# A tile of its own for the ring's last slot, and a new order for every engine, in a fused attention and MLP kernel

## The chip, the cores and the metric

The kernel runs on one core of a Trainium2 chip. The metric is device time in microseconds (us): the median of three runs was 1024.15 us (1023.66 to 1025.81).

Five engines work side by side, each through its own queue in order: TensorE (PE, with PEld for its weight loads), VectorE (DVE), ScalarE (ACT), GpSimd (POOL) and SyncE (SP), which here only issues transfers (DMA). An instruction that waits holds up all that stands behind it on its engine.

## The reference

Eight batches of eight heads go through a linear attention with exponential features; its output, as 4608 tokens of 512 numbers, goes through two dense layers with a squared ReLU between them.

```python
def phi(x):                                   # x: (8, 8, 576, 64), w_phi: (64, 128)
    proj = np.einsum('bhsd,df->bhsf', x, w_phi)
    proj = proj - np.max(np.abs(proj), axis=-1, keepdims=True)
    return np.concatenate([np.exp(proj), np.exp(-proj)], axis=-1)
q_p, k_p = (phi(q), phi(k))
kv = np.einsum('bhsf,bhsd->bhfd', k_p, v)
z = np.sum(k_p, axis=2)
num = np.einsum('bhsf,bhfd->bhsd', q_p, kv)
den = np.einsum('bhsf,bhf->bhs', q_p, z)[..., None] + 1e-06
x = (num / den).transpose(0, 2, 1, 3).reshape(4608, 512)
h = x @ w_in                                  # w_in: (512, 2048)
r = np.maximum(h, 0.0)
return (r * r) @ w_out                        # w_out: (2048, 512)
```

## The kernel before

**Attention.** The 64 heads go in 32 pairs p. Loads of k, q and v (L524, L525, L487) are issued by SP. The first six pairs (`early`) do it all on PE, DVE and ACT: products for keys and queries (L532, L538, L655, L661), the largest absolute value and its subtraction on DVE (L548 to L562, L666, L668), exponentials on ACT (L554, L556), key by value (L594, L599, L627), turns (L639, L689), numerators (L708) and denominators (L725). The other 26 pairs (`visit`, `late`) take other routes: L809, L818, L830 on PE, and POOL for the largest value (L906) and the denominators' sum (L927). For each batch the scale needs the largest of v: ACT L493, DVE L498, then PE L341 (`power`).

**Weights.** The 16 pieces of w_in and w_out (`raw0i` to `raw7o`, L383) come in during the first 110 us. ACT, POOL (L402) and DVE (L406) turn each into two or three parts of lower precision.

**Token ring.** The attention's output is split into a high and a low f16 part (L783, L786) and lies in a ring of eight slots of 256 tokens each, T = 256. In the code, `ring[0]` holds slots 0 to 2 and `ring[1]` slots 3 to 7, one tile of shape [128, 2, 4, 1280]:

```python
def place(slot, t=0):
    half = slot * T >= HR
    return int(half), slot * T + t - HR * half
```

**Dense layers.** The tokens go in 18 chunks of 256. Chunks 0 to 3 (`moe`) take the first product straight (L956, 24 matmuls for each of eight pieces f, reading the ring), and `ph` through the ReLU (ACT L965 or DVE L967) to squares `gh`, `gl` (L973, L975, L249), then the second product (L993, 12 matmuls into `po`). From chunk 4 on they go in pairs of chunks with seven products in place of eight (`step`, L1161, 42 matmuls each; sums on DVE L1167 and L1119). That needs block sums of w_in: `ahead` makes them for all eight f while chunks 0 to 3 are computed, with slot 7 of the ring as its workspace (DVE L1075, L1060, L249; ACT L1079 or DVE L1080; store L1082). They are loaded back by `weights` (L1091, L1093) for each step. Finished `po` banks are scaled into `o` by ACT (L1016) or DVE (L1014) and stored.

**Order.** All work is added to a plan as items, each with an engine, a length, and for a transfer two numbers (`xfer`, `land`). Two strings of digits, ORDER and WAYS, were found by annealing against that plan. ORDER gives the order in which all items are issued, WAYS the engine of each item that may run on several. The kernel doesn't reorder anything at run time. Where the plan shows PE idle, a few matmuls on zeros (`zeros`, L1332) are put in.

Of the kernel before, what the change touches and what calls it, by code (L numbers as in the profile page):

```python
# [26 lines left out]
F = 128  # L27
# [153 lines left out]
def place(slot, t=0):  # L181
    half = slot * T >= HR
    return int(half), slot * T + t - HR * half
# [52 lines left out]
def tile_kernel(ctx, tc, qp, kp, vp, w_phi, w_in, w_out, out):  # L236
# [30 lines left out]
    ring = [[cp.tile([128, KT, HR], F16, name=f"ring0_{i}") for i in range(2)], None]  # L267
# [57 lines left out]
    ld_w = P.add("SP", 0.45, lambda: SP.dma_start(wraw, w_phi), [], [], -100.0, land=2.2, xfer=0.5)  # L325
# [160 lines left out]
    def load_v(p, rank):  # L486
        v_load[p] = P.add("SP", 0.47, lambda: SP.dma_start(v_at(p), vp[p]), [], [v_key(p)], rank, land=2.4, xfer=1.0 if p < 2 else 0.8)  # L487
# [35 lines left out]
    def loads(p, rank):  # L523
        k_load[p] = P.add("SP", 0.47, lambda: SP.dma_start(k_[p], kp[p]), [], [("k", p)], rank, land=2.4, xfer=1.0 if p < 2 else 0.72)  # L524
        q_load[p] = P.add("SP", 0.47, lambda: SP.dma_start(q_[p], qp[p]), [], [("q", p)], rank + 0.5, land=2.4, xfer=0.9 if p < 1 else 0.72)  # L525
# [79 lines left out]
    def early(p):  # L605
# [113 lines left out]
        def dens():  # L719
# [16 lines left out]
            R(5.7), land=2.1, xfer=0.1)  # L736
# [4 lines left out]
    def denominators(p, dens, rows, rank):  # L741
# [5 lines left out]
        o = P.add("SP", 0.4, lambda: SP.dma_start(rd_[p], rc_[p]), [o], [("rc", p), ("rd", p)], rank, land=2.4, xfer=0.1)  # L747
# [3 lines left out]
    def spread(p, o, rows, rank):  # L751
# [4 lines left out]
        dens_of[p] = P.add("SP", 1.3, work, [o], [("rd", p), ("rb", p)], rank, land=2.1, xfer=0.8)  # L756
# [118 lines left out]
    def turn(p, v, key, src, rank):  # L875
# [3 lines left out]
            td_[p].rearrange("s p x -> p s x"), kvs_[p][:, 0:256].rearrange("p (s x) -> p s x", s=2)), [o], [("kvs", p), ("td", p)], rank, land=1.9, xfer=0.1)  # L879
# [3 lines left out]
            [o], [("td", p), ("kz", p)], rank, land=2.2, xfer=0.5)  # L883

    def late(p):
# [4 lines left out]
        w = P.add("SP", 0.4, lambda: SP.dma_start(zd_[p], z4_[p]), sums[p], [("z4", p), ("zd", p)], R(RZ), land=1.9, xfer=0.1)  # L890
# [12 lines left out]
        for h in range(2):  # L903
# [27 lines left out]
                [home, ("den", p)], R(RQ + 1.0), land=2.4, xfer=0.1))  # L931
# [73 lines left out]
    def store(c, v, i, use, bank, g2, Q):  # L1005
# [14 lines left out]
        for k, x in enumerate([slice(0, DM)]):  # L1020
# [6 lines left out]
                  land=1.8, xfer=0.7)  # L1027
# [37 lines left out]
    def ahead(f, rank):  # L1065
# [4 lines left out]
        for k in range(2):  # L1070
            of = lambda x, h, k=k: w_[f][0][:, x, 2 * h + k, :].rearrange("p (j c) -> p j c", j=2)

            def fill(of=of):
                for h in range(2):
# [8 lines left out]
                      [o], [], rank, land=2.0, xfer=0.8)  # L1083
# [5 lines left out]
    def weights(f, rank):  # L1089
        b = in_pair["step"] = in_pair.get("step", 1) ^ 1  # L1090
        o = P.add("SP", 0.45, lambda: SP.dma_start(wo_at(b), wd_[f][0]), [w_stored[f]] + read_o[b], [WO[b]], rank, land=2.4, xfer=1.8)  # L1091
        if f in s_stored:
            s = P.add("SP", 0.45, lambda: SP.dma_start(ws_at(b).rearrange("p k n x c -> p k (n x c)"), wd_[f][1]), s_stored[f] + read_s[b], [WS[b]], rank, land=2.4, xfer=1.8)  # L1093
# [16 lines left out]
        s_stored[f] = [P.add("SP", 0.45, lambda: SP.dma_start(wd_[f][1], ws_at(b).rearrange("p k n x c -> p k (n x c)")), [s], [WS[b]], rank, land=2.0, xfer=1.4)]  # L1110
# [110 lines left out]
    def put_away(n, k, f, g, rank):  # L1221
# [4 lines left out]
        gone[k, f] = P.add("SP", 0.9, work, [g] + read_back.get((k - 2, f), []), [("gh", n), ("gl", n)], rank, land=2.2, xfer=1.9)  # L1226

    def take_back(n, k, f, rank):
# [4 lines left out]
        o = P.add("SP", 0.9, work, [gone[k, f]], [("gh", n), ("gl", n)], rank, land=2.4, xfer=1.6)  # L1233
# [64 lines left out]
    for k, cs in enumerate(PAIRS):  # L1298
# [3 lines left out]
        for i in range(2):  # L1302
            add_x(cs, i, used, m - 6.0 + 0.5 * i, None if k else RT[0])
# [61 lines left out]
    "#m#s$+$/$3#B#R#z#X#|$:$M$O$%$;$?$d$s$v%,%1%0%:%;%A%F%Y%[%n%}&&&+![#[#6#d#A#E$$$1#H#L#p$-#u#w$)$I$<$K"
    "$V$h$m$4$b$k$o$r$y%#%&%+%-%/%6%@%C%^&%%t&*%O%U%X%g%k%y&.&4&8!d!^#;$D#F#Q$!$Z&f(%(+(b)A#U$=#h$2$#$.$N"
    "$W$&$9$B$F$7$8$J$L$q$z%(%?%L%%%2%=%7%>%E%J%K%d%i%o%q%z&!&6&;&D&`&(&-&1&=&@&S&q)%))(n).#n${$E$a$P$Y$j"
    "%5$S$^$e$p$f$i$u%e%T%h%p&,&<&2&?&M&I&P&C&_&a&T&[&^&c&h&k(1(5(I(P(D(N(Q(e(h)*)>)S)q)V)s$@%_%H%B%Q%R%`"
    "%x%V%Z%f%l%N%c%]%v%|&#&)%I&v(8&o%{(>(@(F&p&y(^&u&}(((0(&(2(6(G&5(,($(J(B(K(c&Z(o(t)<(s({)!)&)?)C)F)Y"
# [107 lines left out]
```

## Time and profile before

| | |
|---|---|
| median of three runs | 1024.15 us |
| the profiled execution | 1026.95 us |
| its span, first to last instruction | 1025.1 us |
| PE busy | 999.6 us, 98% |
| DVE / ACT / POOL busy | 799.8 / 604.3 / 357.1 us |
| mean granted PE clock | 0.991 of full speed |

The profiled execution is 2.8 us above the median; 1.85 us of it lie around the span. Idle time in a row below is what an engine waited before an instruction, with what ended the wait behind the arrow. A busy PE is modelled from the ends of pipelined matmuls.

### The profile page before, as it was taken

What the parts mean: (1) busy time and instruction counts of PE and PEld (TensorE: products, weight loads), DVE (VectorE), ACT (ScalarE), POOL (GpSimd) and SP (SyncE); (2) the same over time, 40 slices, a digit from 0 to 9 for tenths busy, and PEclk for the clock granted to TensorE, in tenths of its full rate; (3) what the DMA queues carried; (4) which work ended last, traced back from release to release, by engine and by line L of the source; (5) the groups of instructions that cost most, each with busy time, mean ns of one, the idle gap of its engine ahead of it and who ended that gap; (6) DMA issues with size and microseconds to landing.
All of it is one profiled execution on the core that took longest, in us unless ns stands there. A gap on an engine that the chain in (4) does not pass through costs nothing.

```text
span 1025.1 us, 19857 instructions
## 1 busy us (share of the span) xinstructions
PE 999.6 (98%) x7548; PEld 679.8 (66%) x7548; DVE 799.8 (78%) x1407; ACT 604.3 (59%) x1131; POOL 357.1 (35%) x144
## 2 busy tenths in 40 slices
PE   7999999999999999999999999999999999999998
PEld 4656666666667776677657776677667757767674
DVE  5898789899798788988789888777897776672443
ACT  5888766677554478377764876456735642440423
POOL 1562355565420064444274444431543420000000
PEclk9899999999999999999999999999999999999999
DMA  8863433564225576679476776757656765674321
GB/s 314 289 208 126 148 81 108 146 172 134 46 67 169 192 231 165 215 215 266 155 207 184 213 236 179 226 165 239 166 148 197 218 187 197 194 255 143 110 93 42
DMA packets 155687, 180.60 MB, mean 176 GB/s; under 512 B 76872, under 2 KB 105544, under 8 KB 153544
## 3 DMA queue, kind: packets, MB, share of 16 engines
q1 hardware_dynamic: 155304, 178.81, 57.2%
q8 instruction: 59, 0.97, 0.4%
q10 hardware_dynamic: 288, 0.52, 0.1%
q14 instruction: 36, 0.29, 0.1%
HBM read 137.93 MB, written 41.21 MB: 175 GB/s over the span
## 4 chain that ended last, share of the span: by engine, by line
PE 80%; DVE 7%; DMA 5%; issue 3%; ACT 2%; POOL 2%; SPq 1%; POOLq 0%; DVEq 0%; ACTq 0%
PE po L993 30%; PE ph L1161 10%; PE pn L1161 6%; PE pv L1161 6%; PE ph L956 6%; PE pz L594 4%; PE pn L830 3%; PE pp L1161 2%; PE pn L809 2%; PE pp L532 2%; PE pv L830 2%; DMA q<-in_qp_dram 1%; DMA rb<-rd 1%; PE pz L599 1%; PE pv L993 1%
## 5 line engine op out<-in xcount | busy, mean ns | idle before, releaser
L1161 PEld LDWEIGHTS <-w 128*128 128x128 f16 x2352 | 224.3, 98 | 48.4 <-issue 20.7
L906 POOL PARTITION_ALL_REDUCE mx<-pt x52 | 116.1, 2233 | 204.9 <-ACT pt L253 119.0
L993 PE MATMUL po<-wh,gh 128*128 128x512 f32 x544 | 175.2, 443 | 0.0
L927 POOL PARTITION_ALL_REDUCE rb<-rb x26 | 97.2, 3740 | 161.9 <-DVE rb L924 154.4
L993 PE MATMUL po<-wl,gh 128*128 128x512 bf16 x544 | 141.0, 381 | 1.8 <-DVE o L1014 1.5
L1212 ACT ACTIVATE w<-w,cw 128x512 f32<-128x512 f32 x112 | 78.6, 714 | 107.7 <-DVE w L1167 107.7
L993 PE MATMUL po<-wl,gl 128*128 128x512 bf16 x544 | 140.4, 380 | 0.6 <-DVE gl L249 0.4
L993 PEld LDWEIGHTS po<-wh,gh 128*128 128x128 f32 x544 | 103.3, 190 | 31.8 <-issue 0.3
L927 POOL PARTITION_ALL_REDUCE ds<-ds x26 | 96.1, 3698 | 39.1 <-DVE ds L924 20.8
L973 ACT ACTIVATE gh<-w 128x512 fp32r<-128x512 f32 x112 | 69.9, 625 | 62.4 <-PE po L993 30.0
L993 PEld LDWEIGHTS <-gl 128*128 128x128 bf16 x576 | 56.3, 98 | 69.2 <-DVE gl L249 1.6
L249 DVE TENSOR_TENSOR gl<-w,gh 128x512 bf16<-128x512 f32 x112 | 80.6, 727 | 23.9 <-ACT w L975 23.1
L956 PE MATMUL ph<-ring,w 128*128 128x256 f16 x768 | 91.1, 276 | 2.8 <-DVE r L967 2.3
L993 PEld LDWEIGHTS <-gh 128*128 128x128 bf16 x576 | 51.2, 98 | 59.4 <-issue 21.5
L956 PEld LDWEIGHTS <-w 128*128 128x128 f16 x768 | 73.5, 99 | 22.9 <-issue 12.1
L1161 PE MATMUL ph<-ring,w 128*128 128x256 f16 x624 | 85.6, 273 | 0.0
L1161 PE MATMUL pv<-w,w 128*128 128x256 f16 x576 | 70.7, 273 | 0.3 <-ACT pt L253 0.3
L580 DVE TRANSPOSE_TENSOR_REDUCE z<-e 128x32 f32<-128x1024 f32 x52 | 64.0, 1233 | 3.8 <-ACT e L556 3.2
L1167 DVE TENSOR_TENSOR w<-pv,w 128x512 f32<-128x512 f32 x96 | 53.1, 553 | 10.2 <-PE pv L1161 8.1
L554 ACT ACTIVATE e<-e 128x512 f32<-128x512 f32 x64 | 39.5, 622 | 29.3 <-DVE e L551 29.2
L249 DVE TENSOR_TENSOR qe<-pt,mx 128x576 f32<-128x576 f32 x52 | 45.6, 878 | 10.1 <-POOL mx L906 5.5
L1167 DVE TENSOR_TENSOR w<-pn,w 128x512 f32<-128x512 f32 x48 | 32.9, 686 | 23.3 <-PE pn L1161 14.1
(256 smaller groups left out, 1835.3 us busy)
## 6 DMA issues: line engine op xcount, KB each, us to landing
w<-wd SPq DMA_DIRECT2D x112, 512.0 KB, 4.4
gd<-gh SPq DMA_DIRECT2D x48, 256.0 KB, 4.2
gh<-gd SPq DMA_DIRECT2D x48, 256.0 KB, 3.2
v<-in_vp_dram SPq DMA_DIRECT2D x32, 320.0 KB, 3.9
q<-in_qp_dram SPq DMA_DIRECT2D x32, 288.0 KB, 4.0
k<-in_kp_dram SPq DMA_DIRECT2D x32, 288.0 KB, 3.7
rb<-rd SPq DMA_DIRECT2D x64, 144.0 KB, 3.6
out_dram<-o SPq DMA_DIRECT2D x34, 256.0 KB, 4.1
```

The source lines that it names most:

```text
L249: eng.tensor_tensor(out=out_, in0=a, in1=b_, op=ALU.subtract)
L580: sums[p].append(P.add("DVE", dve_us(256 * k), lambda: V.tensor_reduce(out=col(), in_=src().rearrange("p k (b x) -> p k b x", x=32), op=AL ...
L594: PE.matmul(out=to[64 * h:64 * h + 64, 0:256], lhsT=v_at(p)[:, t, h, :], rhs=e_[2 * p + h][:, t].rearrange("p s f -> p (s f)"), start=t == ...
L830: PE.matmul(out=to[64 * h:64 * h + 64, :], lhsT=kz_[n][:, 128 * s_ + 64 * h:128 * s_ + 64 * h + 64], rhs=qe_[2 * n + h].rearrange("p (s x) ...
L906: o = P.add("POOL", par_us(S), lambda n=n, h=h: G.partition_all_reduce(mx_[n - EARLY], pt_[p][:, h, :], channels=128, reduce_op=bass_isa.R ...
L927: o = P.add("POOL", 3.6, lambda y=y: G.partition_all_reduce(y(), y(), channels=128, reduce_op=bass_isa.ReduceOp.add), [o], [home], R(RQ + ...
L956: PE.matmul(out=ph[:, j, :], lhsT=w_[f][0][:, w, t, 128 * j:128 * j + 128], rhs=at_ring(c, x, t), start=k == 0, stop=k == 3 * KT - 1)
L973: sq = P.add("ACT", act_us(512), lambda: A.activation(out=gh_[n], in_=r(), func=AF.Square), after, use + [("gh", n)], Q)
L993: PE.matmul(out=bank(i), lhsT=x[:, j, 128 * i:128 * i + 128], rhs=w[:, j, :], start=turn + j + s == 0, stop=(turn, j, s) == (NFP - 1, 1, 2))
L1161: PE.matmul(out=to, lhsT=fl(x, *al)(k), rhs=fr(y, *ar)(k), start=n == 0, stop=n == 5)
L1167: V.tensor_tensor(out=to, in0=a, in1=b, op=ALU.add)
L1212: x = P.add("ACT", act_us(512, 1), lambda i=i: A.activation(out=r()[:, 2 * i:2 * i + 2, :], in_=r()[:, 2 * i:2 * i + 2, :], func=AF.Relu, ...
```

## The change

It has five parts.

1. Slot 7 of the ring becomes a tile of its own (`ring[2]`, shape [128, 2, 4, 256]); `ring[1]` keeps slots 3 to 6. A pair's output that crosses from slot 6 to slot 7 is now cut in two there, which is the case for batches 3 and 6: eight more high and eight more low pieces.
2. The lengths that the plan gives to transfers (`xfer`, `land`) are new numbers. They change no instruction by themselves.
3. In `add_x` of the first pair of chunks the second half waits for the first.
4. ORDER and WAYS are new throughout.
5. WAYS moves some items: `wh` casts (L442) from POOL 7 to 4 and on DVE 1 to 3, `wl` casts (L460) on POOL 2 to 4, scaling of `po` on ACT (L1016) 20 to 24 and on DVE (L1014) 14 to 10. Zero matmuls (L1332) go from 10 to 14, and four of them now stand right behind PE's first eight (L359).

```diff
 def place(slot, t=0):
-    half = slot * T >= HR
-    return int(half), slot * T + t - HR * half
+    half = (slot * T >= HR) + (slot == RING // T - 1)
+    return half, slot * T + t - (0, HR, RING - T)[half]
...
-        whole = late_pool.tile(
-            [128, 2, KT, RING - HR], F16, name="ring1")
-        ring[1] = [whole[:, i] for i in range(2)]
+        for x, size in ((1, RING - HR - T), (2, T)):
+            whole = late_pool.tile([128, 2, KT, size], F16, name=f"ring{x}")
+            ring[x] = [whole[:, i] for i in range(2)]
...
-        k_load[p] = P.add("SP", 0.47, lambda: SP.dma_start(k_[p], kp[p]), [], [("k", p)], rank, land=2.4, xfer=1.0 if p < 2 else 0.72)
+        k_load[p] = P.add("SP", 0.47, lambda: SP.dma_start(k_[p], kp[p]), [], [("k", p)], rank, land=1.85, xfer=1.02)
...
-        o = P.add("SP", 0.45, lambda: SP.dma_start(wo_at(b), wd_[f][0]), [w_stored[f]] + read_o[b], [WO[b]], rank, land=2.4, xfer=1.8)
+        o = P.add("SP", 0.45, lambda: SP.dma_start(wo_at(b), wd_[f][0]), [w_stored[f]] + read_o[b], [WO[b]], rank, land=1.9, xfer=1.76)
...
-            add_x(cs, i, used, m - 6.0 + 0.5 * i, None if k else RT[0])
+            add_x(cs, i, used + ([] if k or not i else [parts_x[cs, 0]]), m - 6.0 + 0.5 * i, None if k else RT[0])
...
-    "!&!#!!!(!)!4!:!1!6!O!_!j!m!p!s)x!+!J!I!P!S!7!X!W!a!v#K#N#T#c#g#k!Y#!!{#(#-#5#J!>#&!i#+#1###j#P#q#v#{"
+    "!$!#!!!(!)!+!9!4!=!M!`!e!g!j$7&q!,!P!N!V![!-!X!W!^!w#>#B#]#d#I#p!a#!###)#-#4#M!?#&!p#,#1!{#o#S#u#y$!"
```

**Place 1: SP's first transfers.** Before, SP's queue begins like this (`raw0i`, `raw1i`, `raw2i` are pieces of w_in):

```order
L525 DMA q_167<-in_qp_dram 128x576
L524 DMA k_169<-in_kp_dram 128x576
L325 DMA wraw<-in_w_phi_dram 128x768
L487 DMA v_172<-in_vp_dram 128x640
L487 DMA v_174<-in_vp_dram 128x640
L524 DMA k_176<-in_kp_dram 128x576
L383 DMA raw0i<-in_w_in_dram 128x2048
L524 DMA k_218<-in_kp_dram 128x576
L487 DMA v_220<-in_vp_dram 128x640
L383 DMA raw1i<-in_w_in_dram 128x2048
L487 DMA v_231<-in_vp_dram 128x640
L383 DMA raw2i<-in_w_in_dram 128x2048
```

The next row is the load of the second pair's q. Of the change:

```order
L325 DMA wraw<-in_w_phi_dram 128x768
L525 DMA q_168<-in_qp_dram 128x576
L524 DMA k_170<-in_kp_dram 128x576
L487 DMA v_172<-in_vp_dram 128x640
L487 DMA v_174<-in_vp_dram 128x640
L524 DMA k_176<-in_kp_dram 128x576
L487 DMA v_178<-in_vp_dram 128x640
L383 DMA raw0i<-in_w_in_dram 128x2048
L383 DMA raw1i<-in_w_in_dram 128x2048
L524 DMA k_225<-in_kp_dram 128x576
L487 DMA v_232<-in_vp_dram 128x640
L525 DMA q_235<-in_qp_dram 128x576
```

`wraw` now goes first, `raw1i` stands ahead of the third k (whose buffer must first be read by PE), and the second q stands ahead of `raw2i`.

**Place 2: DVE in `ahead`, while PE computes chunk 3 from slot 3.** Before, with the semaphores that each instruction waits for in brackets (`w_0_1242` is a piece of w_in, `ring_1719` the tile of slots 3 to 7):

```order
L551 TENSOR_TENSOR e_3458<-pp_3424,km_3456 128x4x128 [waits DVE_49]
L1075 TENSOR_TENSOR ring_1719<-w_0_1242 128x2x128 [waits PE_49] x2
L761 TENSOR_TENSOR rb_3033<-n_3234,rb_3033 128x576 [waits DMAHW1_49,DMAHW0_49]
L1060 TENSOR_TENSOR ring_1719<-ring_1719 128x128 [waits DVE_49]
L249 TENSOR_TENSOR ring_1719<-ring_1719 128x128 [waits DVE_49] x3
L786 SCALAR_TENSOR_TENSOR ring_1719<-rb_3033,cb,ring_1719 128x576 [waits Activation_49]
```

Of the change, at the same step (`ring_1682` is slot 7's own tile, `ring_1681` holds slots 3 to 6):

```order
L249 TENSOR_TENSOR qe_3476<-pt_3310,mx_3403 128x576 [waits Pool_49]
L1075 TENSOR_TENSOR ring_1682<-w_0_1248 128x256 x2
L1060 TENSOR_TENSOR ring_1682<-ring_1682 128x128 [waits DVE_49]
L249 TENSOR_TENSOR ring_1682<-ring_1682 128x128 [waits DVE_49] x3
L898 TENSOR_REDUCE zc_3504<-kz_3405 128x4 [waits DMAHW5_49,DMAHW0_49]
L551 TENSOR_TENSOR e_3506<-pp_3412,km_3443 128x4x128
L786 SCALAR_TENSOR_TENSOR ring_1681<-rb_2959,cb,ring_1681 128x576 [waits Activation_49]
```

Of the 32 instructions of L1075, 13 waited for PE before, and none does now. In the other direction, 14 matmuls that read slots 3 to 6 waited for one of L1075 before, and none does now.

**Place 3: DVE and ACT where the last pair with put-away squares ends (about 911 to 919 us).** Before, DVE:

```order
L976 TENSOR_TENSOR w_1_4086<-w_1_4086 128x512
L249 TENSOR_TENSOR gl_10855<-w_1_4086,gh_10849 128x512
L249 TENSOR_TENSOR gl_10870<-w_1_4086,gh_10853 128x512
L249 TENSOR_TENSOR r<-r 128x256 x4
L1053 CAST w_1_3656<-r 128x1024
L1014 TENSOR_SCALAR o_10887<-po_10348,cc 128x512
```

DVE of the change, and behind it ACT of the change:

```order
L249 TENSOR_TENSOR gl_10875<-w_1_4083,gh_10869 128x512
L249 TENSOR_TENSOR gl_10890<-w_1_4083,gh_10873 128x512
L249 TENSOR_TENSOR r<-r 128x256 x4
L1053 CAST w_1_3742<-r 128x1024
L249 TENSOR_TENSOR w_1_3742<-r,w_1_3742 128x1024
```

```order
L973 ACTIVATE gh_10873<-w_1_4083 128x512
L975 ACTIVATE w_1_4083<-w_1_4083 128x512
L1016 ACTIVATE o_10902<-po_10367,cc_79 128x512
L1016 ACTIVATE o_10909<-po_10370,cc_79 128x512
L1052 ACTIVATE w_1_3882<-r 128x1024
```

Before, ACT scaled the first of these two `po` banks and DVE the second, behind the sums for the next pair; now ACT scales both, one after the other.

Two more moves on PE: around 20 us the second pair's eight L655 now stand ahead of L639 and L341, which before came first, and around 39 us four numerator matmuls (L708) now stand between L538 and L661, which before followed each other directly.

## Rows read from the trace of the kernel before

**Rows 1.** The page's first part: busy us, share of span, instructions, per engine.

```profile
PE 999.6 (98%) x7548; PEld 679.8 (66%) x7548; DVE 799.8 (78%) x1407; ACT 604.3 (59%) x1131; POOL 357.1 (35%) x144
```

**Rows 2.** Windows: stretch, its us, busy us per engine, clock, DMA share, GB/s.

```profile
150.00:200.00 50.00, 48.68 (x378) 33.46 (x377) 46.31 (x83) 32.61 (x67) 27.33 (x10) 1.00 0.43 120
400.00:500.00 100.00, 99.96 (x738) 67.53 (x735) 88.03 (x151) 66.27 (x131) 44.96 (x15) 1.00 0.71 214
```

**Rows 3.** Windows of PE alone: stretch, its us, PE busy, clock, DMA, GB/s.

```profile
7.00:14.00 7.00, 6.83 (x58) 0.76 0.79 296
24.00:29.00 5.00, 5.00 (x39) 0.66 1.03 419
41.00:47.00 6.00, 5.94 (x46) 0.72 0.50 107
86.00:90.00 4.00, 2.36 (x28) 1.00 0.24 74
287.00:291.00 4.00, 4.00 (x22) 0.57 0.01 4
918.50:923.00 4.50, 4.50 (x15) 0.62 0.80 273
```

**Rows 4.** Waits of PE, whole span: us in total, times, longest.

```profile
PE pn L341 <- DVE m L498: 2.8, 2, 1.6
PE ph L655 <- DMA wraw<-in_w_phi_dram: 2.4, 1, 2.4
PE ph L956 <- DVE r L967: 2.3, 3, 1.6
PE pn L725 <- ACT n L253: 1.6, 1, 1.6
PE po L993 <- DVE o L1014: 1.5, 1, 1.5
...
PE pn L538 <- DVE pt L668: 1.0, 1, 1.0
PE pn L661 <- DVE et L562: 1.0, 1, 1.0
...
PE ph L655 <- DMA q<-in_qp_dram: 0.5, 1, 0.5
```

**Rows 5.** The chain that ended last, 0 to 30 us: start, us, what.

```profile
1.64 5.09 DMA wraw<-in_w_phi_dram
...
13.09 10.78 DMA q<-in_qp_dram
```

**Rows 6.** Timeline of DVE around 21 us.

```profile
21.11 1.23 DVE L406 SCALAR_TENSOR_TENSOR u<-u,raw1i 128x1024 int32<-128x1024 int32 x1 [1.53 <-POOL raw1i L402]
...
22.72 0.15 DVE L498 TENSOR_REDUCE m<-vm 128x1 f32<-128x4 f32 x1
```

**Rows 7.** Timeline of DVE, 278 to 288 us.

```profile
278.21 0.42 DVE L1075 TENSOR_TENSOR ring<-w 128x256 f32<-128x256 f16 x1 [1.99 <-PE ph L956]
...
284.90 0.75 DVE L967 TENSOR_SCALAR r<-ph,cw 128x512 f32<-128x512 f32 x1
285.57 1.01 DVE L1075 TENSOR_TENSOR ring<-w 128x256 f32<-128x256 f16 x1
```

**Rows 8.** Timelines of PE and POOL there.

```profile
286.63 0.60 PE L956 MATMUL ph<-ring,w 128*128 128x256 f16 x4 [0.42 <-DVE ring L1075]
...
283.46 3.90 POOL L927 PARTITION_ALL_REDUCE rb<-rb  x1 [7.61 <-DVE rb L924]
```

**Rows 9.** Timelines of ACT, DVE and PE, 915 to 919 us.

```profile
915.29 0.69 ACT L1016 ACTIVATE o<-po,cc 128x512 f32<-128x512 f32 x1 [1.11 <-PE po L993]
...
917.27 0.81 DVE L1014 TENSOR_SCALAR o<-po,cc 128x512 f32<-128x512 f32 x1
...
918.12 0.38 PE L993 MATMUL po<-wl,gh 128*128 128x512 bf16 x1 [1.50 <-DVE o L1014]
```

**Rows 10.** Transfers: times issued, KB each, median us from issue to landing.

```profile
w<-wd SPq DMA_DIRECT2D x112, 512.0 KB, 4.4
```

More of the change, by code (lines that the diff above doesn't have):

```diff
@@ L266, in tile_kernel @@
     wout = [[None] * 3 for _ in range(NFP)]
-    ring = [[cp.tile([128, KT, HR], F16, name=f"ring0_{i}") for i in range(2)], None]
+    ring = [[cp.tile([128, KT, HR], F16, name=f"ring0_{i}") for i in range(2)], None, None]
     cc = cp.tile([128, NT // 128], F32, name="cc")
@@ L323, in tile_kernel @@
         V.memset(mask[64 * h:64 * h + 64, h, :], 1.0)
-    ld_w = P.add("SP", 0.45, lambda: SP.dma_start(wraw, w_phi), [], [], -100.0, land=2.2, xfer=0.5)
+    ld_w = P.add("SP", 0.45, lambda: SP.dma_start(wraw, w_phi), [], [], -100.0, land=1.7, xfer=1.36)
     pool_start = P.add("POOL", 10.8, lambda: None, [], [], -100.0)
@@ L735, in early @@
             den_[p], dn()[0:128:32, :].rearrange("j (r x) -> j r x", x=9)), [o], use + [("den", p)],
-            R(5.7), land=2.1, xfer=0.1)
+            R(5.7), land=1.5, xfer=0.1)
         rows = lambda h: rd_[p].rearrange("(c h r) x -> h c (r x)", c=2, h=2)[h].unsqueeze(0).to_broadcast([64, 2, SH])
@@ L754, in work @@
                 SP.dma_start(rb_[p][64 * h:64 * h + 64, :].rearrange("p (c x) -> p c x", c=2), rows(h))
-        dens_of[p] = P.add("SP", 1.3, work, [o], [("rd", p), ("rb", p)], rank, land=2.1, xfer=0.8)
+        dens_of[p] = P.add("SP", 1.3, work, [o], [("rd", p), ("rb", p)], rank, land=1.85, xfer=1.7)
     def tokens(p, nums, rank):
@@ L888, in late @@
         R = lambda x: rank + x
-        w = P.add("SP", 0.4, lambda: SP.dma_start(zd_[p], z4_[p]), sums[p], [("z4", p), ("zd", p)], R(RZ), land=1.9, xfer=0.1)
+        w = P.add("SP", 0.4, lambda: SP.dma_start(zd_[p], z4_[p]), sums[p], [("z4", p), ("zd", p)], R(RZ), land=1.25, xfer=0.36)
         back = []
@@ L1026, in store @@
             P.add("SP", 0.38, lambda x=x: (SP if whole else A).dma_start(out[128 * tt:128 * tt + 128, x], home(x.start)), [o], [mine], Q,
-                  land=1.8, xfer=0.7)
+                  land=1.35, xfer=0.6)
     parts_x, in_pair = {}, {}
@@ L1082, in ahead @@
             o = P.add("SP", 0.45, lambda k=k: SP.dma_start(wd_[f][1].rearrange("p x (n c) -> p x n c", n=4)[:, k], ring[spot][1][:, :, c0:c0 + T]),
-                      [o], [], rank, land=2.0, xfer=0.8)
+                      [o], [], rank, land=1.35, xfer=0.8)
             in_pair["ahead"] = [o]
@@ L1224, in work @@
             SP.dma_start(gd_[k % 2][f][1], gl_[n])
-        gone[k, f] = P.add("SP", 0.9, work, [g] + read_back.get((k - 2, f), []), [("gh", n), ("gl", n)], rank, land=2.2, xfer=1.9)
+        gone[k, f] = P.add("SP", 0.9, work, [g] + read_back.get((k - 2, f), []), [("gh", n), ("gl", n)], rank, land=1.5, xfer=1.2)
     def take_back(n, k, f, rank):
@@ L1231, in work @@
             SP.dma_start(gl_[n], gd_[k % 2][f][1])
-        o = P.add("SP", 0.9, work, [gone[k, f]], [("gh", n), ("gl", n)], rank, land=2.4, xfer=1.6)
+        o = P.add("SP", 0.9, work, [gone[k, f]], [("gh", n), ("gl", n)], rank, land=1.5, xfer=1.42)
         read_back[k, f] = [o]
@@ L1365 @@
[L1365 to L1369, printed above, removed]
```

177 lines of the change are left out of this document (91 added, 86 removed).

## The prediction

> **What bounds the kernel now.** I read the engines' totals first: PE is busy for 999.6 of 1025.1 us, and the next engine, DVE, for 78% [rows 1]. The windows say that this is no average over unlike stages: between 400 and 500 us PE is idle for 0.04 us, and even at 150 to 200 us, while weights and attention are still being prepared, for 1.3 us [rows 2]. So nearly every part of the program is bound by PE's own stream of matmuls, which the change doesn't shorten. What it can move is the 25.5 us in which PE stands idle, and what they bring with them.
>
> What they bring is seen in windows over PE alone [rows 3]. In five stretches the granted clock is below full speed; 7 to 14 us ran at 0.76, which loses 0.24 x 7.0 = 1.7 us, and the other four lose 0.34 x 5 = 1.7, 0.28 x 6 = 1.7, 0.43 x 4 = 1.7 and 0.38 x 4.5 = 1.7 us. Of TensorE's two levels, 2.4 and 1.2 GHz, the chip granted the lower one for a part of each, and the sum is 8.5 us. What PE did before each is in its waits [rows 4]: 2.4 us for `wraw`; 1.6 us at L341, with the second q after it; 1.0 and 1.0 us at L661 and L538; 1.6 us behind L967 with 0.42 us more [rows 8]; 1.5 us at L993. The single wait of 1.6 us at L725 was followed by full clock (86 to 90 us) [rows 3, 4]. So a wait that is near another, or longer than this one, costs about 1.7 us beside itself, and one of up to 1.6 us that stands alone does not.
>
> **The change part by part.**
>
> *Start.* `wraw` was issued at 1.64 us and landed 5.09 us later [rows 5]; PE waited 2.4 us for it [rows 4]. It now goes first in SP's queue, two issues earlier. A transfer's place decides what shares the way with it: only `wraw` and q must land before PE's L655, k no longer. The gain is between 0 (all three land together as before) and 1.6 us (`wraw` leaves at the span's start); I take 0.7, which is k's part of the three (576 of 1920 words a partition) of the 2.4 us. Four zero matmuls stand in the wait that is left; at the 0.38 us of a 128x512 matmul [rows 9] they last 1.5 us, so the wait covers them, and if it shrank to nothing they would cost that. With PE occupied for most of it I expect the low clock at 7 to 14 us to be shorter: 0 to 1.7, taken as 1.2. Sum 1.9.
>
> *Around 21 us.* PE waited 1.6 us at L341 for DVE's L498, which ended at 22.87 us; DVE stood before it in L406 until the part of `raw1i` was there (1.53 us idle, then 1.23 us of work) [rows 4, 6]. `raw1i` now passes one k and one v in SP's queue. The k waits for a buffer that PE reads, so this is more than two issues; how far ahead it comes is bounded by the transfers on the way. The second q landed 10.78 us after its issue [rows 5], behind `raw1i` and `raw2i`, of which one is now behind it and the other well ahead; and L655 covers the rest of PE's wait. The wait of 1.6 and the 0.5 for q [rows 4] can go, and 1.7 of low clock with them: 0 to 3.8, taken as 3.0, because L341 still comes after a join of `raw1i` on DVE.
>
> *Around 39 us.* Two waits of 1.0 us, at L661 and L538 [rows 4]. Four L708 now stand in the first; the second has nothing new in front of it. If a single one is left, the low clock of 41 to 47 us should go too, by what L725 showed. 0 to 2.7, taken as 1.7.
>
> *The ring's last slot.* PE waited 1.6 us for L967 on DVE, and 0.42 us more for an L1075 of `ahead` [rows 4, 8]. L967 started at 284.90, in line behind items that had slid back when DVE stood idle for 1.99 us at 278.21, waiting for PE's L956 [rows 7]. L956 reads slot 3 and L1075 writes slot 7; they share nothing but the tile. The two engines thus waited for each other in turn, and with a tile apart neither does. Had DVE not lost those 1.99 us, L967 would have started about 2 us earlier, more than PE's 1.6. It could gain the 0.42 alone, or 1.6 + 0.4 + 1.7 of clock = 3.7; I take 2.7, since DVE's line there is a new one.
>
> *End of the last put-away pair.* PE waited 1.5 us for a `po` bank that DVE scaled at 917.27, while ACT had scaled the other from 915.29 to 915.98 [rows 9]. Both are now ACT's, one behind the other: the second would end at about 915.98 + 0.69 + a hop, some 916.7 in place of 918.08, so 1.3 of the 1.5 go, and 1.7 of low clock [rows 3]. 0 to 3.2, taken as 2.8.
>
> *What costs nothing.* Eight more cuts of the ring make eight more DVE and ACT pieces, each shorter than L967's 0.75 us [rows 7], and three or four weight items move from POOL to DVE, of 1.2 us or less as L406 [rows 6]. Their cover is DVE's spare time, 12 us in 100 at 400 us, 3.7 in 50 at 150 us [rows 2]; if it is gone there, they cost up to what they last, some 4 us.
>
> *What a new order gives back.* The sum so far is 1.9 + 3.0 + 1.7 + 2.7 + 2.8 = 12.1 us; by the upper ends it is 3.3 + 3.8 + 2.7 + 3.7 + 3.2 = 16.7. But the order is new on every engine, and the waits of before show that such an order can leave some of its own. I put in two lone waits like L725's (2 x 1.6) and one pair with its low clock (2.0 + 1.7): 6.9 us, between 0 and the 14.4 that the four pairs of before cost (waits of 2.1 + 2.0 + 2.0 + 1.5, clock 4 x 1.7). Net 12.1 - 6.9 = 5.2.
>
> The profiled execution took 1026.95 us and would take 1021.8; the median of the runs is 2.8 us lower, and so I predict 1024.15 - 5.2 = **1019.0 us**.
>
> **A rule against the fourth part.** At 285.57 one L1075 took 1.01 us where the one at 278.21 took 0.42, with POOL inside L927 from 283.46 on [rows 7, 8]. The Trainium skill (SBUF — State Buffer, "Who interferes with whom") has a rule on this: a DVE instruction with two SBUF inputs and a GpSimd instruction that reads SBUF exclude each other, and the later one stands until the other ends. Here L1075 was slower by 0.6 us, not by the 1.8 us that L927 still had to run, so the trace bears the rule out in part.
>
> **The rivals.**
>
> *The port, not the tile, made DVE late at 285 us.* Then PE's wait for L967 stays, and the ring gives only its 0.42. For it: the 0.6 us above. Against: DVE's 1.99 us of idle is three times as much, and comes before. 1019.0 + 2.7 - 0.4 = 1021.3. The rule of the Trainium skill is this case at full strength.
>
> *The waits only move.* Nearly all of the 12.1 comes back at other places: 1022.1 to 1026.2, about 1024. For it: both orders were found against a plan's lengths, and the four pairs of before lay at four unlike places. Against: three of the five causes (`raw1i` late, a tile shared, a bank on the busy engine) are gone from the queues themselves (places 1 to 3).
>
> *Slower: weights come late.* The plan now lets a load of `w` take 0.45 + 1.76 + 1.9 = 4.1 us from issue where it had 4.65; the median was 4.4 [rows 10]. Before, no load of `w` held PE up. 112 loads serve 56 steps. Where the new order has used the difference up, a step waits some 0.3 us; it decides from 18 steps on (18 x 0.3 = 5.4 us, the whole net gain), and at all 56 it is 17 us. With two thirds of them, 11 us: 1019.0 + 11 = 1030.
>
> *Little comes back.* The 12.1 less one lone wait of 1.6: 1024.15 - 10.5 = 1013.7; by the upper ends, and nothing back, 1024.15 - 16.7 = 1007.5.
>
> **How the numbers follow.** As forecast (1015 to 1022): 0.45. Port (1021): 0.08. Little comes back (1007.5 to 1015): 0.15. Waits only move: 0.18. Slower: 0.14. The likeliest gives 1019.0. The range reaches up over the waits that move and about half of the slower case, to 1028, and down to 1009, near the upper ends' 1007.5: it leaves out some 0.08 above and 0.04 below, and the rest of the 2 in 10 for a cause not listed. A measurement of this kernel tells 0.2%, 2 us, from no change: faster 0.68 (the first three cases), same 0.17 (most of the fourth), slower 0.15.
>
> **What would show it.** In the new trace: L655 first at about 6.1 us; no wait of PE over 1 us at L341 near 21 us, and full clock at 24 to 29 us; one wait at most near 39 us; no wait of DVE's L1075 for PE, none of L956 for L1075, and full clock near 290 us; `po` banks free by ACT near the end of the put-away pairs, and full clock after. Wrong would be: PE idle for over 25 us in all, a window at 150 to 900 us with more than 1.5 us idle in 50, or waits of PE's L1161 for `w<-wd`.

## The result

The changed kernel takes 1009.94 us (median of 4 runs, 1007.7 to 1010.36), the kernel before 1024.53 us beside it: ratio 0.9852, interval 0.9834 to 0.9871. It is faster by 14.6 us (13.2 to 17.0), where 5.2 were forecast. The direction was right and the time lies in the range, but the gain is nearly three times what the sum gave.

The profiled executions are 1026.95 us before and 1009.59 us after; their spans differ by 17.3 us. The first part of the page after (busy us, share of span, instructions):

```profile
PE 993.1 (99%) x7552; PEld 676.4 (67%) x7552; DVE 801.9 (80%) x1417; ACT 605.3 (60%) x1140; POOL 352.5 (35%) x141
```

Beside [rows 1] PE is idle for 14.7 us in place of 25.5, and 6.5 us less busy, though four more zero matmuls run: that is the clock, which was low for four stretches fewer. The other engines do the same work in the same time, within 5 us. Windows over PE alone, at the places of [rows 3] (us, PE busy, clock, DMA, GB/s):

```profile
7.00:14.00 7.00, 6.56 (x66) 1.00 1.02 418
24.00:29.00 5.00, 5.00 (x89) 1.00 1.02 426
36.00:41.00 5.00, 5.00 (x36) 0.66 0.64 184
...
285.00:290.00 5.00, 5.00 (x36) 1.00 0.41 127
905.00:910.00 5.00, 4.97 (x24) 1.00 1.02 330
```

Four of the five stretches at low clock are gone; the one near 39 us is still there (0.34 x 5 = 1.7 us). The waits of PE, beside [rows 4] (us in all, times, longest):

```profile
PE pn L661 <- DVE et L562: 1.7, 1, 1.7
PE pp L532 <- DVE ds L924: 1.4, 2, 0.7
PE pn L359 <- DVE o L319: 1.2, 1, 1.2
PE pn L708 <- DVE pt L668: 0.9, 1, 0.9
PE pn L538 <- DVE pt L668: 0.8, 1, 0.8
PE po L993 <- DMA gh<-gd: 0.6, 1, 0.6
PE pn L1161 <- DVE n L254: 0.5, 1, 0.5
...
PE po L993 <- ACT o L1016: 0.3, 1, 0.3
```

No wait for `wraw`, none at L341, none of L956 for L1075, and 0.3 us at the end of the last put-away pair. The wait at L359 is PE's first, the same before (1.17 us). Beside it one wait is over 1 us, at L661, and it is the very pair that the third term wanted to shorten. The rows around it, of DVE, POOL and PE in this order (start, us, what; idle before):

```profile
30.79 1.13 DVE L348 TENSOR_SCALAR pw<-pw 128x2 int32<-128x2 int32 x1
31.96 1.04 DVE L351 TENSOR_SCALAR cw<-pw 128x2 f32<-128x2 f32 x1
33.04 0.17 DVE L352 RECIPROCAL cw<-cw 128x2 f32<-128x2 f32 x1
...
34.02 0.29 DVE L562 TENSOR_TENSOR et<-pn,kmt 128x128 f32<-128x128 f32 x1
...
30.74 1.16 POOL L402 TENSOR_SCALAR raw3i<-raw3i 128x1024 int32<-128x1024 uint32 x1
31.94 1.04 POOL L460 CAST wl<-u 128x1024 bf16<-128x1024 f32 x1
...
34.46 0.44 PE L661 MATMUL pn<-wraw,q 128*64 128x128 f32 x4 [1.74 <-DVE et L562]
35.70 0.44 PE L538 MATMUL pn<-wraw,k 128*64 128x128 f32 x4 [0.80 <-DVE pt L668]
```

Two instructions on two elements a partition took 1.13 and 1.04 us, and each ends within 0.03 us of POOL's instruction above it (31.92 and 31.90, 33.00 and 32.98). A third of the same size took 0.17. So some 1.8 us of DVE's lateness there look like POOL's, and PE's wait is 1.74; an experiment below moves POOL away.

### The profile page after: what moved, and what is told of

Its sections match the earlier page's. It is cut to its first block, busy times and chain, and to the rows that moved or that the text cites. A ratio compares the mean times of both kernels' runs of the same rounds, so it can differ in the third digit from the quotient of the medians.

```text
span 1007.8 us, 19886 instructions
## 1 busy us (share of the span) xinstructions
PE 993.1 (99%) x7552; PEld 676.4 (67%) x7552; DVE 801.9 (80%) x1417; ACT 605.3 (60%) x1140; POOL 352.5 (35%) x141
## 4 chain that ended last, share of the span: by engine, by line
PE 82%; DVE 7%; issue 4%; DMA 2%; ACT 2%; POOL 1%; SPq 0%; POOLq 0%; DVEq 0%; ACTq 0%
PE po L993 32%; PE ph L1161 9%; PE ph L956 7%; PE pv L1161 6%; PE pn L1161 6%; PE pz L594 4%; PE pn L830 2%; PE pp L532 2%; PE pp L1161 2%; PE pn L809 2%; PE pv L830 2%; POOL rb L927 1%; PE pz L599 1%; PE pv L993 1%; PE pn L993 1%
## 5 line engine op out<-in xcount | busy, mean ns | idle before, releaser
L1161 PEld LDWEIGHTS <-w 128*128 128x128 f16 x2352 | 224.5, 98 | 49.5 <-issue 23.0
L956 PE MATMUL ph<-ring,w 128*128 128x256 f16 x768 | 89.4, 273 | 0.6 <-ACT r L965 0.4
L1161 PE MATMUL ph<-ring,w 128*128 128x256 f16 x624 | 85.6, 273 | 0.0
L956 PEld LDWEIGHTS <-w 128*128 128x128 f16 x768 | 72.9, 98 | 17.9 <-issue 9.9
L1161 PE MATMUL pv<-w,w 128*128 128x256 f16 x576 | 70.8, 273 | 0.3 <-ACT pt L253 0.3
L911 ACT ACTIVATE qe<-qe 128x576 f32<-128x576 f32 x52 | 35.3, 679 | 31.4 <-DVE qe L249 29.7
L976 DVE TENSOR_TENSOR w<-w 128x512 f32<-128x512 f32 x33 | 23.4, 711 | 36.6 <-ACT gh L973 36.5
```

The lines of the kernel that those rows point to most:

```text
L956: PE.matmul(out=ph[:, j, :], lhsT=w_[f][0][:, w, t, 128 * j:128 * j + 128], rhs=at_ring(c, x, t), start=k == 0, stop=k == 3 * KT - 1)
L1161: PE.matmul(out=to, lhsT=fl(x, *al)(k), rhs=fr(y, *ar)(k), start=n == 0, stop=n == 5)
```

## Theories

*Lone waits.* The sum of the five terms was about right, and what is wrong is the charge for new waits: the old order's lone waits, which no term named, went as well. *The tile*: sharing it cost more than one pair of waits. *Transfers*: the old order's waits hang on the place of single loads in SP's queue. *Pace*: they hang on the whole order, and a wait that is taken out comes back further on.

All times below are medians; beside them the kernel before had 1024.4 to 1024.8.

## Experiments: the order by stages

Four kernels take the new order and the new engines up to a point (the seam) and the old ones behind it, slot 7 being a tile of its own throughout. The edit itself exchanges digits of ORDER and WAYS; written as code it is:

```diff
-issue = new_order
+issue = [x for x in new_order if x in first] + [x for x in old_order if x not in first]
```

**The tile alone, in the old order.** The edit is part 1 of the change without parts 2 to 5.

> The old order with the old plan numbers and only slot 7 as a tile of its own (eight more high and eight more low pieces, each right behind the piece that it was cut from, on the same engine). If the fourth part of the prediction holds (DVE's idle 1.99 us for L956 made L967 late), the waits of 1.55 and 0.42 us near 285 us go, and with them the low clock of 287 to 291 us: 1.6 + 0.4 + 1.7 = 3.7 us at most, 2.7 as taken, so 1020.8 to 1021.8 against 1024.5, and no wait of L1075 for PE. Rival one, DVE is late there for another reason (POOL's L927, the items in line): the wait for L967 stays, at most 0.42 us, 1024.1. Rival two, the shared tile cost more than that one pair, all along 150 to 300 us (the new kernel gains 6.2 us between 90 and 320 us): about 1018.5.

Measured: 1022.68 us, ratio 0.998 (0.9961 to 0.9998), 1.7 us faster (0.2 to 4.0). Waits of PE, and a window over it:

```profile
PE ph L956 <- DVE r L967: 0.8, 2, 0.7
PE ph L956 <- ACT r L965: 0.7, 1, 0.7
...
287.00:291.00 4.00, 3.97 (x25) 1.00 0.00 0
```

The waits of 1.55 and 0.42 us are gone. One of 0.7 us for ACT stands at 292 us, as in three other kernels of the old order (0.85 to 1.11 us). No L1075 waits for PE. So the mechanism of the fourth term was right for the waits, and sharing the tile cost no more than that. The full clock is not shown to be the tile's. Those three kernels (both banks on ACT, two lone waits, five transfers) keep the shared tile and both waits, and their clock stayed full as well, here the first:

```profile
288.00:292.00 4.00, 4.00 (x29) 1.00 0.01 4
```

In the 12 runs of this kernel the time missing from full clock averages 5.5 us, in those of the kernel before 4.9.

**The same tile shared, in the new order.**

```diff
-        for x, size in ((1, RING - HR - T), (2, T)):
-            whole = late_pool.tile([128, 2, KT, size], F16, name=f"ring{x}")
-            ring[x] = [whole[:, i] for i in range(2)]
+        whole = late_pool.tile([128, 2, KT, RING - HR], F16, name="ring1")
+        ring[1] = [whole[:, i, :, 0:RING - HR - T] for i in range(2)]
+        ring[2] = [whole[:, i, :, RING - HR - T:RING - HR] for i in range(2)]
```

> The changed kernel with its order, cuts and numbers, but slot 7 again in one tile with slots 3 to 6. If the tile is what the gain near 285 us hangs on, DVE and PE wait for each other again: 0.4 to 3.7 us slower than the changed kernel, 1010.3 to 1013.6, with waits of L1075 for L956 and of L956 for L1075. Rival, the new order keeps the two apart by itself: 1009.9, with no such wait on PE. If the tile was worth more than one pair: 1014 or more.

Measured: 1009.93 us (1008.53 to 1015.46), the changed kernel's time. DVE waits for PE again (4.8 us in all in the kernel before):

```profile
DVE ring L1075 <- PE ph L956: 2.9, 3, 1.7
```

Yet no wait of L956 is over 0.41 us: PE doesn't need what DVE does there so soon. So in the new order the tile is worth nothing that can be measured; the stall that it cured in the old order is cured by the order too.

**New up to 60, 145 and 300 us.**

> The seam moved to about 60 us, where the two orders hold nearly the same items on either side (7 of 307 differ); zero matmuls as in the changed kernel, slot 7 its own tile. The changed kernel is 5.0 us ahead at 70 to 75 us. If the gain up to there is kept: 1022.7 (the tile alone) - 5.0 = 1017.7. If a lead on PE at that point is lost on what the old order does behind it, as with the seam at 90 us: 1022 to 1023.

> The seam at about 145 us, behind the last weights. Of the 12.9 us that the changed kernel is ahead at the first L1161, its traces put 3.5 behind 150 us (waits of 0.53, 0.65, 1.55 and 0.42 and low clock 1.7, against waits of 0.68 and 0.69), and 2.5 of these come back with the tile alone. So 1022.7 - 9.4 = 1013.3 if the gains up to 145 us are kept, and they are then the first three terms and the lone waits of 60 to 150 us. If the seam loses them, 1018 or more. Together with the seam at 300 us (1013.3 measured) the first would say that the order between 145 and 300 us is worth nothing beside the tile.

> New order and engines up to about 300 us, the old behind that. The changed kernel is 12.9 us ahead at the first L1161 (312.1 against 325.0). If the gains add up: 1024.5 - 12.9 = 1011.6, with the waits of before left behind 300 us (1.50 us with low clock near 915 us, and some of 0.3 to 0.8 us). Rival, the seam gives back: 1015 or more. If nothing behind 300 us mattered, it would equal the changed kernel, 1009.9.

Measured against the kernel before: 1020.92 us (faster by 3.8; 2.2 to 6.3), 1016.18 (8.5; 5.3 to 11.4) and 1013.34 (11.1; 7.7 to 12.7). Beside the tile's 1.7 and the whole change's 14.6, the stages so give 2.1, 4.7, 2.6 and 3.5 us, each with an uncertainty of two or three. All three fall short of what was expected, that at 60 us by 3.2 (1017.7), that at 145 us by 2.9 (1013.3) and that at 300 us by 1.7 (1011.6), so a seam may have a price of its own, and the split is rough. By the medians the stage from 60 to 145 us has the largest part, though not by more than the uncertainty; the prediction had no term in it. With the seam at 60 us the old order behind it shows what was lost there (waits of PE, then the chain that ended last):

```profile
PE pn L725 <- ACT n L253: 2.2, 1, 2.2
...
PE pv L594 <- ACT kz L253: 1.9, 1, 1.9
...
77.61 5.09 DMA rb<-rd
...
82.95 1.41 POOL rb L761
...
84.38 0.42 ACT n L253
...
84.84 1.16 PE pn L725 x13
```

PE's wait is read from the bottom: ACT can't copy n until POOL has used the old n, and POOL stands still until `rb<-rd` has landed, 5.09 us after its issue.

**Seams at 90 us, both ways.**

> New order, engines and zero matmuls up to about 90 us, the old order and engines behind that, with slot 7 as its own tile throughout. The changed kernel is 6.7 us ahead at 82 us (the fifth pair's L725 starts at 81.99, before at 88.69). If its gains lie where they are seen and add up, 1024.5 - 6.7 less what the tile gives behind 90 us (2.7 to 3.7): 1014.1 to 1015.1. Rival, the old order behind it depends on what stood ahead of it and gives part back at the seam: 1017 or more. If the prediction's first three terms were all that this stretch had (1.9 + 3.0 + 1.7 = 6.6) and 3 us of new waits came back, it would be 1018.

> The reverse of the seam at 90 us: the old order, engines and zero matmuls up to the same 80 items of PE, the new behind that, slot 7 its own tile. If what the changed kernel gained up to 90 us (6.7 us) is worth that much at the end, 1009.9 + 6.7 = 1016.6. If what comes behind 90 us decides and a lead there is lost on what follows (as in the run with the new order first, which was 7.9 us ahead at 81 us and 1.3 at 142 us), 1011 to 1013. With a seam that costs as much as that one did (6 us): 1020 or more, and then the seam, not the order, is what both runs show.

Measured: 1022.35 us (2.1 below the kernel before, interval 0.9974 to 1.0005) and 1024.74 (0.998 to 1.0021): no difference is shown for either. The first was 7.9 us ahead at 81 us and 1.5 at 142; the second gains nothing from the new order behind 90 us. They can't both be right about the stage, so the seam itself costs there, as the second expectation allowed. The first's rows of PE show where:

```profile
94.57 0.66 PE L689 MATMUL pp<-ident,pt 128*128 128x128 f32 x4 [1.28 <-ACT qe L700]
97.02 1.69 PE L809 MATMUL pv<-q,wraw 64*128 64x512 f32 x2 [0.68 <-ACT n L253]
100.35 4.68 PE L956 MATMUL ph<-ring,w 128*128 128x256 f16 x24 [1.65 <-DVE r L967]
```

From 97 to 104 us its clock is low, too, which loses 3.4 us. In the second a wait of 4.64 us stands at an L956 at 108 us, with low clock from 107 to 113 us. The two orders differ at that place in 14 of 419 items, loads and POOL's weights among them. These two runs say nothing of the order.

## Experiments: one wait at a time

**Both banks on ACT, in the old order.**

```diff
 L1016 ACTIVATE o_10880<-po_10345,cc_79 128x512
-L1014 TENSOR_SCALAR o_10887<-po_10348,cc 128x512
+L1016 ACTIVATE o_10887<-po_10348,cc_79 128x512
```

> The kernel before with one instruction moved: the second po bank at the end of the last put-away pair is scaled by ACT (L1016) behind the first, and no longer by DVE (L1014). By the fifth part of the prediction 1.3 of the 1.50 us at 918 us go: 1024.4 - 1.3 = 1023.1, and 1021.4 where the low clock of 918 to 923 us goes with it. Rival, PE waits as long for the next item of DVE (the sums for the next pair): 1024.4.

Measured: 1024.84 us, ratio 0.9996 (0.9981 to 1.0012): no difference. Rows of ACT and PE, and a window over PE:

```profile
917.17 1.26 ACT L1016 ACTIVATE o<-po,cc 128x512 f32<-128x512 f32 x2 [1.11 <-PE po L993]
...
917.91 1.17 PE L993 MATMUL po<-wl,gh 128*128 128x512 bf16 x4 [0.31 <-ACT o L1016]
925.70 1.47 PE L1161 MATMUL pp<-w,w 128*128 128x256 f16 x12 [0.40 <-DVE w L249]
...
918.00:924.00 6.00, 6.00 (x30) 1.00 0.85 276
```

The 1.50 us are gone as the fifth term said, 0.40 come back at the next pair; the median doesn't show the 1.1 that are left, which its interval allows.

**Two lone waits of the old order.** ACT's L493 behind two copies, DVE's L786 ahead of one join:

```diff
-L493 ACTIVATE sx_831,vm_531<-v_767 128x640
 L253 ACTIVATE n_842<-pn_819 128x288
 L253 ACTIVATE n_842<-pv_833 128x288
+L493 ACTIVATE sx_831,vm_531<-v_767 128x640
```

> The kernel before with two items moved on their engines: ACT's L493 (which stood still 1.64 us until its v had landed, near 58 us) goes behind the two copies of n, which PE's L538 at 60.5 us waits for; and DVE's L786 of the first pair's ring goes ahead of the join L406, so that the transfer rb<-rd, for which POOL's L761, ACT's copy of n and PE's L725 at 88.7 us wait, starts 1.4 us sooner. If the lone waits of the old order are losses that can be taken out one by one, the 1.30 us at L538 go and about 1.4 of the 1.64 us at L725: 1024.4 - 2.7 = 1021.7. Rival, a lone wait only stands for the engines' pace there, and PE waits as long a few instructions on: 1024.4, with a wait at L689 or the next L538.

Measured: 1023.35 us, 1.1 below by the medians, with an interval of 0.9982 to 1.002: no difference. In the timeline of PE:

```profile
60.80 1.51 PE L594 MATMUL pv<-e,v 128*64 128x256 f32 x12 [0.68 <-ACT kz L253]
...
86.20 1.18 PE L725 MATMUL pn<-qe,kz 128*32 128x288 f32 x16 [1.14 <-ACT n L253]
```

The wait at L538 went, and half of it came back at PE's next need of ACT, the copy of kz, which stands behind L493 and two L554 and ends at 60.74 us. At L725 it is 1.14 in place of 1.64.

**Five transfers of the old order.** SP's queue alone, here its first part:

```diff
+L325 DMA wraw<-in_w_phi_dram 128x768
 L525 DMA q_167<-in_qp_dram 128x576
 L524 DMA k_169<-in_kp_dram 128x576
-L325 DMA wraw<-in_w_phi_dram 128x768
...
+L383 DMA raw1i<-in_w_in_dram 128x2048
 L524 DMA k_218<-in_kp_dram 128x576
```

> The kernel before with five transfers moved in SP's queue and nothing else: wraw goes first; raw1i ahead of the third k; the second q ahead of raw2i; the seventh v ahead of raw3o; the q of 742 us ahead of one of kz. If the waits that the chains put down to these transfers hang on their place in the queue: part of the 2.4 us for wraw, the 1.65 us at L341 and the 0.5 us for q with the low clock of 24 to 29 us (1.7), the 1.30 us at L538 near 60 us and the 0.79 us near 747 us go, 3 to 7 us in all, 1017.7 to 1021.7. If the engines' pace sets them, PE waits as long a few instructions on: 1023 to 1025.

Measured: 1023.67 us, ratio 0.9986 (0.9970 to 1.0002): 1.1 us, at most 3.1. Waits of PE:

```profile
PE pn L341 <- DVE m L498: 3.4, 2, 1.9
PE ph L956 <- DVE r L967: 2.5, 3, 1.8
...
PE pn L538 <- DVE et L562: 0.9, 1, 0.9
...
PE ph L1161 <- DMA w<-wd: 0.8, 1, 0.8
```

No wait for `wraw` or q is left, L655 begins at 4.76 us in place of 6.86, and L538 no longer waits for n. But L341 waits 1.89 us near 21 us although `raw1i` passed a k and a v, and others grew; in all the waits of over 0.25 us come to 20.2 us, as much as before. The waits that the chain put down to these transfers hung on their places, and yet the sum of waits stayed. The theory of the transfers falls as an account of the gain.

**The pair near 35 us in the new order.** POOL's instruction on `raw1o`, which has not landed yet, goes ahead of two others, so that POOL stands still while DVE does L348 and L351.

```diff
+L402 TENSOR_SCALAR raw1o<-raw1o 128x1024
 L402 TENSOR_SCALAR raw3i<-raw3i 128x1024
 L460 CAST wl_489<-u_421 128x1024
-L402 TENSOR_SCALAR raw1o<-raw1o 128x1024
```

> The changed kernel with one move: on POOL the part of raw1o (L402) stands ahead of that of raw3i and of one L460; the zero matmuls stay where they were. In the changed kernel PE waits 1.74 us at 34.46 and 0.80 us at 35.70, and runs 36 to 41 us at 0.66. DVE had L348 (1.13 us) and L351 (1.04 us) there, which end with POOL's L402 and L460; L352, the same size, takes 0.17. Theory of the port: POOL now stands still until raw1o lands at about 33.0 us, L348 and L351 take about 0.17 us each, DVE is 1.8 us earlier, the wait at L661 goes, and with a lone wait of 0.8 us left the low clock too: 1009.9 - 1.7 - 1.7 = 1006.5, or 1008.2 if the clock still falls. Rival, DVE is late there by its own line of work: L348 and L351 stay long or the wait stays, 1009.9. Rival, the gain moves to the next wait on the weights, which come later now: 1009 to 1010.

Measured: 1012.8 us, 2.9 slower than the changed kernel. The zero matmuls did not stay: the planner had put six in front of L661, where they waited 1.23 us for ACT. A wait of 2.3 us for ACT near 54 us, with low clock behind it, stands there as well. DVE's two instructions took 0.17 us each. With the zeros held in place:

> The move of raw1o once more, now with the zero matmuls where the changed kernel has them. (In the run before, the planner had put six of them in front of L661, and they waited 1.23 us for ACT's copy of n; DVE's L348 and L351 took 0.17 us each there, in place of 1.13 and 1.04.) Theory of the port: L562 ends 1 to 1.8 us earlier against PE's line, the 1.74 us at L661 go, the 0.80 at L538 stay: 1009.9 - 1.7 = 1008.2, and 1006.5 where the low clock of 36 to 41 us goes too. Rival, the weights and what hangs on POOL come later by as much, and PE waits for them near 50 to 60 us: 1009.9 or more.

Measured: 1009.35 us (1007.33 to 1010.8). Rows of DVE, POOL and PE, and a window over PE:

```profile
30.66 0.17 DVE L348 TENSOR_SCALAR pw<-pw 128x2 int32<-128x2 int32 x1
30.86 0.17 DVE L351 TENSOR_SCALAR cw<-pw 128x2 f32<-128x2 f32 x1
...
33.27 1.16 POOL L402 TENSOR_SCALAR raw1o<-raw1o 128x1024 int32<-128x1024 uint32 x1 [2.75 <-DMA raw1o<-in_w_out_dram]
...
32.65 0.44 PE L661 MATMUL pn<-wraw,q 128*64 128x128 f32 x4
...
36.00:41.00 5.00, 4.52 (x77) 1.00 0.98 281
```

The 1.74 us and the low clock are gone, as the theory of the port had it, and L562 ends 1.8 us earlier: POOL made DVE late. The low clock stood behind this pair of waits in the profiles of all seven kernels that have it. A rule of the Trainium skill (SBUF — State Buffer, "Who interferes with whom") names `tensor_scalar` among the instructions of DVE that can take the pair of ports it shares with GpSimd and then wait for the whole of GpSimd's instruction; these rows agree. The median moved by 0.6 us only, less than it can tell; 1.0 us of wait for `gh<-gd` and 0.6 for a k stand in that trace.

**No zeros at the start.**

```diff
-    for n, (t0, t1) in enumerate(gaps):
+    for n, (t0, t1) in enumerate(gaps[1:], 1):
```

> The changed kernel without the four zero matmuls behind PE's first eight. In the changed kernel PE is busy from 1.17 to 7.7 us without a break, and 7 to 14 us runs at full clock. If it is the zeros that keep the clock, PE idles some 1.5 us before L655, the low clock of 7 to 14 us is back (1.7 us), and L655 begins no earlier than 5.9 us: 1009.9 + 1.7 less at most 0.4 = 1011.2 to 1011.6. If the earlier landing of wraw alone did it: full clock without them, 1009.5 to 1009.9.

Measured: 1010.08 us, no difference from the changed kernel, at full clock from 7 to 14 us:

```profile
4.70 0.58 PE L655 MATMUL ph<-wraw,q 64*128 64x128 f32 x1
...
18.95 0.37 PE L655 MATMUL ph<-wraw,q 64*128 64x128 f32 x1 [1.48 <-DMA q<-in_qp_dram]
```

The zeros neither kept the clock nor, in the end, cost anything. `wraw` landed at 3.91 us here and in the changed kernel, and L655 began 1.6 us earlier, behind no zeros; these 1.6 us were lost on the second q.

**All of it together.** SP's second q ahead of `raw1i`, no zeros at the start, `raw1o` first.

> The changed kernel with raw1o first on POOL (1009.35 measured), without the four zero matmuls behind PE's first eight, and with the second q ahead of raw1i in SP's queue. Without the zeros L655 began at 4.70 us and no longer at 6.30, but PE waited 1.48 us for the second q at 18.95, which was issued behind a k that waits for PE. If that q was all that held the 1.6 us up, PE is 1.6 us earlier behind L655 of the second pair: 1009.35 - 1.6 = 1007.7. If raw1i, which now comes 0.5 us later, or k hold PE up there, 1009.4 or more.

Measured: 1009.89 us. L655 begins at 4.92 us, and the lead goes in a wait of 1.7 us for a k near 38 us. No version tried beats the changed kernel by more than the measurement can tell.

## Why the prediction was wrong

**Start: right in size, by another way.** L655 begins 0.56 us earlier (0.7 taken), and 7 to 14 us runs at full clock (1.7; 1.2 taken). But `wraw` landed 2.8 us earlier (3.91 in place of 6.73), beyond the 1.6 that were taken as the most. So the wait did shrink to nothing, and L655 stood behind the four zeros, which last until 6.30 us. It was not the zeros that kept the clock, but the earlier `wraw`: of five profiles with it third in the queue, the low clock stands behind waits of 2.40, 2.43 and 2.90 us and not behind 0.65 and 1.59.

**Around 21 us: right, at its upper end.** 1.65 + 0.51 + 1.7 us are gone, 3.9 against 3.0 taken.

**Around 39 us: wrong.** Waits of 1.74 and 0.80 us with the low clock stand in the place of 0.99 and 1.05: 0.5 us worse, where 1.7 were to be gained. The second wait was rightly seen to have nothing new in front of it. What was missed is POOL beside DVE; of the rivals it is that of the port, at another place.

**The ring's last slot: right in the old order, for the waits.** 1.97 us and 1.7 of clock are gone (3.7 against 2.7), and the tile alone removes the waits. But the order would have done so without the tile, and the 1.7 of clock belong to one execution: three profiles with the same two waits have full clock behind them.

**End of the last put-away pair: right.** 1.5 of the 1.81 us are gone, and 1.7 of clock (3.2 against 2.8), which again most profiles with these waits don't have (last section).

In the profiled executions the five terms so come to 2.3 + 3.9 - 0.5 + 3.7 + 3.2 = 12.6 us, where 12.1 stood.

**What costs nothing: right.** DVE is busy 2.1 us longer, and POOL 4.6 us less. But only two weight items went from POOL to DVE (`wh`, 1 to 3), not three or four.

**The step that failed is "what a new order gives back".** It charged 6.9 us: two lone waits and a pair with its low clock. The pair came, at the old place, and is in the third term. Of lone waits there came more: 15 of 0.15 us or more outside the five places, 6.3 us in all. But the old order had 15 of them too, 9.1 us (1.64 and 0.52 at L725, 1.30 at L538, 1.13 at L341, 0.79 for q and ten smaller), and the new order took these out as well. Four rows of these waits of PE in the kernel before, beside [rows 4]:

```profile
PE pn L538 <- ACT n L253: 1.3, 1, 1.3
...
PE pp L532 <- DVE ds L924: 1.1, 2, 0.6
...
PE pz L818 <- DMA q<-in_qp_dram: 0.8, 1, 0.8
PE pn L725 <- DVE pt L668: 0.5, 1, 0.5
```

I set the new order's full lone waits against an old order with none. The right charge was 6.3 - 9.1 = -2.8 us. With it, 12.1 + 2.8 = 14.9 us come out, 1024.15 - 14.9 = 1009.3 us; 14.6 were measured. In the profiled pair itself 12.6 + 2.8 = 15.4 of the 17.3 us are named so; 1.9 lie in no wait of 0.15 us or more and stay without a name. The stages don't contradict it: the old order's largest lone waits lie between 60 and 150 us, where no term stood and 4.7 us were gained, give or take three.

**Some of this agreement is luck.** The clock was counted from one execution. In 86 runs of the kernel before, beside these experiments, the time went from 1019.6 to 1029.9 us and the mean granted clock from 1.000 to 0.990: the three runs at 0.999 or more took 1019.6 to 1020.4 us, the seven at 0.991 or less 1026.7 to 1029.9. The share of time missing from full clock averages 4.9 us; the profiled execution, at 0.991, is at the low end. The changed kernel loses 1.3 us (four runs). So some 3.6 us of the 14.6 are clock, where the profiled pair shows 6.8: the terms of the ring and of the last put-away pair counted clock that most profiles with these waits don't lose. About 11 are left for the rest; the pair's idle time falls by 10.8 (25.5 to 14.7), of which the four zeros fill 1.7 without saving time.

**What stays open.** Taken out one by one, the waits give little: beside the tile's 1.7 us, the six kernels that remove 1 to 5 us of them, in either order, moved the median by at most 1.1 us. The whole order takes some 11 us out, with the tile shared too. That it does is shown; why it can where single edits can't is not; that it does so because the transfers' new lengths are truer is not: nothing tried separates the new numbers from a second search. A search with the old numbers was not made, nor was the third part of the change tried by itself.

**The rivals.** Waits that only move: not for the order as a whole, but true of nearly every single edit. Weights late: no wait of L1161 for `w<-wd`. Port: not at 285 us, where the tile alone removed the wait, but at 31 us. Little comes back: this is what came, at 0.15.

## What to carry to other kernels

When an order is replaced, count the old order's small waits before charging the new one for its own; both have them, and only the difference is a cost. A stall that the chain names plainly may still give nothing when cured alone, since the engine behind it comes next: test it in the order that will be kept. And take what the clock costs from many runs, not from the one that was profiled.

## What was not expected of the hardware

*The same waits, with and without low clock.* The pair of 0.31 and 1.50 us at the end of the last put-away pair stands in six other kernels; one had the low clock behind it (0.82 and 0.84 in the two windows of 5 us from 910 us, the seam at 90 us), and the tile alone, the seams at 60 and 300 us, the two lone waits and the five transfers had 1.00. After single waits of 1.87 and 2.21 us (the seam at 60 us) the clock stayed full too. The ring's pair of 1.55 and 0.42 us had it in one profile of four. The pair near 39 us had it in five of six, those near 21 us (five profiles) and, in the new order, near 35 us (seven) each time. So "a pair costs 1.7 us" is not a price: some pairs had it each time, others in one or two executions.

*Small instructions held for a microsecond.* L348 and L351 work on two elements a partition, and took 1.13 and 1.04 us beside POOL, 0.17 without.

*A place in the queue, and the spread.* With `wraw` first it landed at 3.71 to 4.53 us (eleven profiles), with it third at 5.28 to 7.35 us (five). PE's first L655 began at 5.42 to 7.48 us in those five, and at 4.70 to 4.92 us in the three that have `wraw` first and no zeros ahead; in the other eight the zeros set it, not the loads.
